# An attention pair on one Trainium2 core: half of each next unit's x loaded one step earlier, in named seats

## The chip, the cores and the metric

The kernel runs on one core of a Trainium2 chip. The metric is device time in microseconds of one execution. Each execution's profile also gives a span, from the first to the last instruction, which is a little shorter than the time.

## The reference

Two attention layers run side by side on inputs of their own, and their outputs are concatenated on the last axis. Each has x of 2048 rows by 1024 columns, a weight wqkv (1024 x 3072), 32 heads of 32 columns, and an output weight wo (1024 x 1024). Everything is float32.

- Layer B: each row attends to itself and the 255 rows before it. `softmax(q k^T / sqrt(32) + mask) v`, then `@ wo`.
- Layer A: each row attends to 8 rows: itself and the rows 2, 4, ..., 14 before it (window 8, dilation 2); then `@ wo`.

## The kernel before

**Units.** The rows are cut into 8 units of 512 rows: units 0 to 3 are layer B's, units 4 to 7 layer A's (whose rows are sorted by parity, so that the dilation becomes a plain window). In each unit the 32 heads go in 8 groups of four, s = 0 to 7. For a unit u and a group s the work is

- `qk(u, s)`: q and k of four heads, two products of 8 steps each (steps over the 1024 columns in pieces of 128),
- attention of the group: scores, row maximum, exponential, sum, values,
- `v(u, part)`: the values' product, in three parts after s = 0, 5 and 7; part 2 (16 steps) comes behind `qk(u, 7)` and is the last reader of the unit's x,
- `o(u, n)`: output projections n = 0 to 7, each contracting the outputs of all eight groups. Those of a layer B unit run in the unit behind it, two each ahead of groups 2 to 5. Those of unit 3 run in units 4 and 5, by the table `O_LATE`. The projections of layer A, and part of its values, run as a Strassen-like product of seven (`PRODUCTS`).

**Precision.** A float32 operand is split into a high part (a cast to a shorter format, lines 247 and 250) and a low part (the rest, a subtraction on VectorE, line 253). A product is three matmuls: high by high, high by low, low by high (`TERMS`). All matmuls are issued at line 295. So every tile of x or of a weight costs one cast, on ScalarE or VectorE, and subtractions on VectorE.

**The stream.** x and the weights are 512 KB items in one list, `items`, loaded in that order into three `raw` buffers (line 192, issued by POOL) and then split into `wpool` (three weight tiles) or x tiles. A raw buffer is filled again when the item three places ahead of the new one has been split. An x item makes two x tiles of 128 partitions by 2 x 512, one unit has eight. There are nine x tiles in rotation (`xpool`) and ten room tiles r0 to r9 (`slot`), which hold attention outputs by `hg % 10` (hg = 8u + s), two late x items of unit 0, and sums later on. `split_to(n)` asks for items up to n to be split. A product asks for the weight after its own at step `ASK` = 2, if that item is no x.

**The order of all instructions** is set while the program is written, by a list scheduler at the end of the function. It keeps four sequences (auxiliary rows, second scores with values, first scores, and `gemm`, the big products in the order of `plan`) and a clock model for each engine (`Clock`); it takes the next instruction group from the sequence that is ready first, and `defer` places follow-up work by modelled times. What the engines wait for on the chip is then semaphores, in the fixed order.

**x at a unit's end.** `x_items(u)` are four steps of no cost that ask for the split of the unit's four x items. They are put among the steps of other products: for unit 1 two of them in `v(0, 2)` and two in `qk(0, 7)`; for units 2 to 6 all four in part 2 of the values of the unit in front, after steps 1, 5, 9 and 13. In the list of items they stand behind the two weights of that part and the first weight of `qk(u, 0)`; the second weight of `qk(u, 0)` stands behind x.

**The start.** `FIRST` lists the pieces of the first six items (four of x, two weights); all nine loads are issued by ScalarE (lines 174 and 177). Ten matmuls on zeros (`WARM`) run before the data is there, and `FILL` puts 1, 9, 1 and 4 more behind steps 1 to 4 of the first product.

**Layer A's evacuation** (`evac_window`): q goes to SBUF at line 550, k at line 555, with 8 columns of the unit in front ahead of k: copied from `tails` by ScalarE (line 558) where there is a unit in front in the same row order, else cleared by VectorE (line 561).

## Time and profile before

| what | value |
|---|---|
| time, median of 3 runs | 1806.21 us (1802.6 to 1809.89) |
| the profiled execution: time | 1805.51 us |
| the profiled execution: span | 1803.8 us |
| TensorE matmuls busy | 1779.3 us, 14505 instructions |
| VectorE busy | 1305.3 us |
| ScalarE busy | 929.7 us |
| POOL busy | 412.1 us |
| granted TensorE clock, mean | 0.999 |
| HBM read, written | 201.33 MB, 53.48 MB |

PE is TensorE's matmul row, PEld its weight loads, DVE VectorE, ACT ScalarE, POOL GpSimd, SP the sync engine. A row of the timeline gives the start and the length in us, the engine, the line, the operation, the tile written and those read, the count, and in brackets the idle time before it and what ended it. Matmuls overlap in the pipeline, so a row of several is shorter than the sum of its instructions. A POOL row of a load is its issue, not the transfer. By the timeline unit 2 begins at about 444 us, units 3 to 7 at 700, 956, 1155, 1335 and 1518; from 1675 on only the last products run.

### The profile page before, as it was taken

What the parts mean: (1) busy time and instruction counts of PE and PEld (TensorE: products, weight loads), DVE (VectorE), ACT (ScalarE), POOL (GpSimd) and SP (SyncE); (2) the same over time, 40 slices, a digit from 0 to 9 for tenths busy, and PEclk for the clock granted to TensorE, in tenths of its full rate; (3) what the DMA queues carried; (4) which work ended last, traced back from release to release, by engine and by line L of the source; (5) the groups of instructions that cost most, each with busy time, mean ns of one, the idle gap of its engine ahead of it and who ended that gap; (6) DMA issues with size and microseconds to landing.
All of it is one profiled execution on the core that took longest, in us unless ns stands there. A gap on an engine that the chain in (4) does not pass through costs nothing.

```text
span 1803.8 us, 38475 instructions
## 1 busy us (share of the span) xinstructions
PE 1779.3 (99%) x14505; PEld 1441.8 (80%) x14505; DVE 1305.3 (72%) x2905; ACT 929.7 (52%) x2310; POOL 412.1 (23%) x951
## 2 busy tenths in 40 slices
PE   9999999999999999999999999999999999999999
PEld 7787777888777888777887778888878787887887
DVE  6777876768867769867678576665766768678866
ACT  4565566555656565656655444423443435356442
POOL 3222323222242223332223400110011101002120
PEclk9999999999999999999999999999999999999999
DMA  8354664644646556455546365675566558858984
GB/s 246 111 151 135 185 166 135 173 139 133 185 140 175 150 135 172 142 158 140 149 115 184 93 196 182 204 207 162 187 210 209 179 185 266 262 177 281 342 288 145
DMA packets 154794, 324.58 MB, mean 180 GB/s; under 512 B 18032, under 2 KB 58992, under 8 KB 154608
## 3 DMA queue, kind: packets, MB, share of 16 engines
q0 software_dynamic: 45792, 166.74, 30.5%
q1 hardware_dynamic: 97728, 134.40, 26.3%
q10 hardware_dynamic: 11088, 20.98, 3.1%
q8 instruction: 115, 1.88, 0.4%
q14 instruction: 71, 0.58, 0.1%
HBM read 201.33 MB, written 53.48 MB: 141 GB/s over the span
## 4 chain that ended last, share of the span: by engine, by line
PE 88%; DVE 4%; issue 3%; DMA 2%; ACT 2%; ACTq 0%; POOL 0%; SPq 0%; POOLq 0%; DVEq 0%
PE g L295 69%; PE s L295 13%; PE o L295 6%; DVE w L253 1%; DMA raw<-xs 1%; DMA raw<-wo 1%; DVE x L253 0%; ACT s L1351 0%; ACT w L247 0%; DMA outs<-ost 0%; ACT wide L1213 0%; DVE band L1174 0%; DMA raw<-wqk 0%; DVE band L1202 0%; DMA qst<-nat 0%
## 5 line engine op out<-in xcount | busy, mean ns | idle before, releaser
L295 PE MATMUL g<-x,w 128*128 128x512 f32 x3552 | 878.6, 393 | 6.1 <-ACT w L247 3.2
L295 PEld LDWEIGHTS g<-x,w 128*128 128x128 f32 x3552 | 654.8, 188 | 137.9 <-issue 6.3
L253 DVE TENSOR_TENSOR w<-raw,w 128x512 fp32r<-128x512 f32 x510 | 334.8, 698 | 47.9 <-ACT w L247 39.1
L1351 ACT ACTIVATE s<-s,nm 128x384 f32<-128x384 f32 (+2 forms) x512 | 274.5, 537 | 106.3 <-DVE nm L1346 100.0
L1346 DVE CUSTOM_DVE_ANT_0 s<-s,mask_d 128x384 f32<-128x384 f32 (+2 forms) x512 | 261.9, 554 | 91.6 <-PE s L295 91.3
L295 PE MATMUL g<-w,x 128*128 128x256 f32 (+1 forms) x1728 | 307.7, 327 | 1.1 <-DVE w L253 0.8
L1410 POOL TENSOR_SCALAR_AFFINE_SELECT pbuf<-pbuf 128x128 f32<-128x128 f32 (+1 forms) x603 | 220.5, 394 | 316.1 <-ACT pbuf L1431 314.2
L295 PEld LDWEIGHTS g<-w,x 128*128 128x128 f32 x1728 | 255.4, 190 | 25.7 <-issue 1.6
L295 PE MATMUL g<-r,w 128*128 128x512 f32 x960 | 239.8, 394 | 1.4 <-ACT r L1306 0.7
L1431 ACT ACTIVATE pbuf<-s 128x384 f32<-128x384 f32 (+2 forms) x480 | 203.3, 505 | 64.6 <-PE s L295 59.8
L295 PEld LDWEIGHTS g<-r,w 128*128 128x128 f32 x960 | 177.0, 188 | 37.4 <-DVE r L1310 1.6
L192 POOL DMA_DIRECT2D raw<-wqk x126 | 68.3, 542 | 406.7 <-DVE w L253 251.8
L295 PEld LDWEIGHTS s<-qst,kst 128*128 128x128 f32 x704 | 113.4, 188 | 42.3 <-ACT s L1351 16.8
L295 PE MATMUL s<-kst,qst 96*128 96x384 f32 (+2 forms) x512 | 142.9, 343 | 0.9 <-ACT s L1351 0.7
L295 PE MATMUL s<-qst,kst 128*128 128x256 f32 (+2 forms) x704 | 137.0, 302 | 4.0 <-ACT s L1351 3.2
L250 DVE CAST w<-raw 128x1024 fp32r<-128x1024 f32 x180 | 124.4, 691 | 19.7 <-PE g L295 19.6
L247 ACT CAST w<-raw 128x1024 fp32r<-128x1024 f32 (+1 forms) x76 | 78.6, 1037 | 84.1 <-PE g L295 32.9
L295 PEld LDWEIGHTS s<-kst,qst 96*128 96x128 f32 x512 | 93.5, 189 | 26.5 <-issue 4.6
L1351 ACT ACTIVATION_READ_ACCUMULATOR s<-s,nm 128x1 f32 x512 | 105.3, 206 | 0.0
L1213 ACT COPY wide<-band 32x512 f32<-32x512 f32 x128 | 79.0, 617 | 40.3 <-DVE band L1204 38.5
L295 PE MATMUL o<-pbuf,vbuf 128*32 128x384 f32 (+2 forms) x1408 | 91.6, 389 | 0.0
L591 ACT ACTIVATE nat<-g 128x512 fp32r<-128x512 f32 x64 | 38.4, 599 | 97.8 <-PE g L295 88.7
(90 smaller groups left out, 1434.0 us busy)
## 6 DMA issues: line engine op xcount, KB each, us to landing
raw<-wqk POOLq DMA_DIRECT2D x126, 512.0 KB, 4.7
raw<-wv POOLq DMA_DIRECT2D x60, 512.0 KB, 4.8
qst<-nat SPq DMA_DIRECT2D x96, 256.0 KB, 4.1
kst<-nat SPq DMA_DIRECT2D x96, 256.0 KB, 5.5
raw<-wo POOLq DMA_DIRECT2D x44, 512.0 KB, 4.7
raw<-xs POOLq DMA_DIRECT2D x28, 512.0 KB, 5.0
outs<-ost ACTq DMA_DIRECT2D x38, 256.0 KB, 2.3
kst<-halo SPq DMA_DIRECT2D x72, 128.0 KB, 4.5
```

Source lines behind the costliest of these rows:

```text
L192: (self.nc.scalar if early else self.nc.gpsimd).dma_start(raw if len(ap.shape) == 2 else raw.rearrange("p (a b) -> p a b", a=2), ap)
L247: nc.scalar.copy(t[:, 0, :], raw)
L250: nc.vector.tensor_copy(t[:, 0, :], raw)
L253: nc.vector.tensor_tensor(t[:, 1, c:c + 512], raw[:, c:c + 512], t[:, 0, c:c + 512].bitcast(F32), op=ALU.subtract)
L295: nc.tensor.matmul(out, left, right, **k)
L591: nc.scalar.activation(hl[:, 0, :], ps, AF.Copy, scale=sc)
L1213: nc.scalar.copy(diag[r:r + 32, :, :, c:c + 32], turned[r:r + 32, :, :, 1, :])
L1346: nc.vector.tensor_tensor_reduce(ps[:, :n], ps[:, :n], mask[:, cut:full], scale=-1.0, scalar=BIG, op0=ALU.add, op1=ALU.min, accum_out=nm)
L1351: nc.scalar.activation(ps[:, :n], ps[:, :n], AF.Exp, bias=nm, scale=-1.0, accum_out=sm)
L1410: nc.gpsimd.affine_select(w, w, pattern=[[0, m], [step, n]], compare_op=ALU.is_ge, fill=0.0, base=base, channel_multiplier=chan)
L1431: nc.scalar.activation(w, ps[:, :pack * n].rearrange("p (j n) -> p j n", j=pack), AF.Exp)
```

## The change

- **x earlier in layer B.** `EARLY_X` moves x items 0 and 1 of units 2 and 3, and item 0 of unit 4, ahead in the list, in front of the weights of the last value part; their splits go into `qk(u, 7)` at its steps 5 and 11 (`EARLY_AT`). The rest stays in the value part, at steps given by `LATE_AT`. As the last weight of `qk(u, 7)` now has x behind it, the first value weight is asked for by a step of its own, 13 (`ASK_V`). Unit 1's two early items stay.
- **Seats.** The x tiles of units 0 to 3 (`X_SEATS`) and the outputs of layer B (`O_SEATS`) have named tiles, out of the same nine x and ten room tiles; layer A's x goes round the nine in the order of `X_RING`. The values of the seventh group of unit 0 wait for the last qk of that unit (its output takes an x tile's seat).
- **Unit 4:** `O_LATE` puts the projections 0 to 3 of unit 3 one group later.
- **Units 5 and 6:** the second weight of `qk(u, 0)` stands between x items 1 and 2. Units 5 to 7 ask for it at step 2 of the first product of `qk(u, 0)`, when x is split.
- **The start:** loads 0 and 2 of the nine stay on ScalarE's queue (`BY_ACT`), seven go to SP; `FILL` is 1 and 5 matmuls behind steps 1 and 2.
- **Tails:** cleared once by POOL, and copied for every unit of layer A; where the next unit has none in front, VectorE clears them after use.
- One ask in front of the seven-part products comes at step 5 in place of 6.

```diff
--- before.py
+++ after.py
@@ -36,7 +36,12 @@
 XAT = 1
-FIRST_X = 2
+EARLY_X = {1: (0, 1), 2: (0, 1), 3: (0, 1), 4: (0,)}
+EARLY_AT, ASK_V = (5, 11), 13
+LATE_AT = {2: {2: 5, 3: 9}, 3: {2: 10, 3: 14}, 4: {1: 3, 2: 10, 3: 14}}
+X_SEATS = ("x0 x1 x2 x3 r0 r2 r1 r4", "x4 x5 x6 x7 x8 x0 x1 x2", "x3 r8 r9 r0 x4 x5 x6 x7", "x2 x8 r2 r3 x3 x4 x5 x6")
+O_SEATS = ("r5 r6 r3 r7 r8 r9 r0 r2", "r1 r4 r5 r6 r3 r7 r2 x8", "x0 x1 r1 r4 r5 r6 r7 r8", "r9 r0 r1 r4 r5 r6 r7 r8")
+X_RING = "x0 x1 x7 x2 x8 x3 x4 x5 x6"
 X1_AT = (2, 9)
@@ -46,7 +51,7 @@
 OUTPUT_OPS = ((3, 2, 3, ALU.add), (2, 0, 2, ALU.subtract), (0, 3, 0, ALU.subtract), (1, 1, 0, ALU.subtract))
-O_LATE = {4: {2: (0, 1), 3: (2, 3)}, 5: {2: (4, 5), 3: (6, 7)}}
+O_LATE = {4: {3: (0, 1), 4: (2, 3)}, 5: {2: (4, 5), 3: (6, 7)}}
 O_AT = {}
@@ -56,7 +61,8 @@
 FIRST = ((0, 0), (1, 0), (0, 1), (2, None), (3, 0), (1, 1), (4, None), (3, 1), (5, None))
-FILL = ((1, 1), (2, 9), (3, 1), (4, 4))
+BY_ACT = (0, 2)
+FILL = ((1, 1), (2, 5))

@@ -167,15 +173,16 @@
                 self.raw[3 + i] = raw, [None, None]
-            for i, h in FIRST:
+            for n, (i, h) in enumerate(FIRST):
                 raw, t = self.raw[i]
                 ap = self.items[i][1]
+                queue, took = (self.nc.scalar, self.ck.load) if n in BY_ACT else (self.nc.sync, self.ck.copy)
                 if h is None:
-                    self.nc.scalar.dma_start(raw.rearrange("p (a b) -> p a b", a=2), ap)
-                    t[:] = [self.ck.load("first", self.ck.now)] * 2
+                    queue.dma_start(raw.rearrange("p (a b) -> p a b", a=2), ap)
+                    t[:] = [took("first", self.ck.now)] * 2
                 else:
-                    self.nc.scalar.dma_start(raw[:, S * h:S * h + S], ap[:, h] if len(ap.shape) == 3 else ap[:, S * h:S * h + S])
-                    t[h] = self.ck.load("half", self.ck.now)
+                    queue.dma_start(raw[:, S * h:S * h + S], ap[:, h] if len(ap.shape) == 3 else ap[:, S * h:S * h + S])
+                    t[h] = took("half", self.ck.now)
             self.loaded = 6
@@ -220,7 +227,7 @@
                 for h in range(2):
-                    t = self.xpool.tile([P, 2, S], F32R, tag="x", name="x") if self.items[i][0] != "xw" else self.sums()
+                    t = self.x_tile(i, h) if self.items[i][0] != "xw" else self.sums()
                     self.ready[i].append(self.parts(t, raw[:, h * S:(h + 1) * S], t0, i < SIDE))
@@ -232,11 +239,6 @@
             self.ck.defer(end, lambda n=i + m + NRAW + 1 if i < NRAW else max(2 * NRAW + m, i + NRAW + deep + 1): self.load_to(n))
-
-    def x_tile(self, i, h):
-        if (i, h) in self.first:
-            return self.slot(self.first[i, h])
-        return self.xpool.tile([P, 2, S], F32R, tag="x", name="x")

@@ -271,7 +273,7 @@
     wpool = ctx.enter_context(tc.tile_pool(name="wpool", bufs=3))
-    xpool = ctx.enter_context(tc.tile_pool(name="xpool", bufs=NX))
+    xpool = ctx.enter_context(tc.tile_pool(name="xpool", bufs=1))
     roomp = ctx.enter_context(tc.tile_pool(name="roomp", bufs=1))
@@ -396,7 +398,7 @@
                     if i == 1 and p[1:] == (0, 2):
-                        unit_x(1, *range(FIRST_X)) if FIRST_X else None
+                        unit_x(1, *EARLY_X[1])
                 else:
@@ -404,10 +406,17 @@
                     item(p + (t,), "w", wqk[ly, 2 * p[2] + t])
+            if 0 < p[1] < DU and p[2] == NG - 1:
+                unit_x(p[1] + 1, *EARLY_X[p[1] + 1])
         else:
...
                 item(("qk", p[1], 0, 0), "w", wqk[units[p[1]][0], 0])
-                unit_x(p[1], *range(FIRST_X if p[1] == 1 else 0, 4))
+                if DU < p[1] < U - 1:
+                    unit_x(p[1], 0, 1)
+                    item(("qk", p[1], 0, 1), "w", wqk[units[p[1]][0], 1])
+                    unit_x(p[1], 2, 3)
+                else:
+                    unit_x(p[1], *[g for g in range(4) if g not in EARLY_X.get(p[1], ())])
             else:
@@ -430,8 +439,21 @@
     st.sums = sums_tile
-    st.first = {(4, 0): 6, (4, 1): 7, (5, 0): 8, (5, 1): 9}
-    st.slot = lambda i: slot(i).rearrange("p (a s) -> p a s", a=2).bitcast(F32R)
+    def place_of(name):
+        if name[0] == "x":
+            return xpool.tile([P, 2, S], F32R, tag=name, name="x")
+        return roomp.tile([P, 1024], F32, tag=name, name="r").rearrange("p (a s) -> p a s", a=2).bitcast(F32R)
+
+    ring = X_RING.split()
+    x_at = {(where["x", u, g], h): X_SEATS[u].split()[2 * g + h] for u in range(DU) for g in range(4) for h in range(2)}
+
+    def x_tile(i, h):
+        if (i, h) in x_at:
+            return place_of(x_at[i, h])
+        ring.append(ring.pop(0))
+        return place_of(ring[-1])
+
+    st.x_tile = x_tile
     last_dense = DU * NG - 1
@@ -471,6 +493,7 @@
                                 base=-8, channel_multiplier=0)
+        nc.gpsimd.memset(tails, 0.0)
         cst["keep_f"] = bands("keep_f", P, BIG, 0.0, (-1, -1, 1))
@@ -554,12 +577,10 @@
                 e = ck.use("act", 0.485, ck.now + ck.SEM)
-                if has_halo:
-                    nc.scalar.copy(qk[:, S:S + 8], tails[:, s, :])
-                    e = ck.use("act", 0.2, e)
-                else:
-                    nc.vector.memset(qk[:, S:S + 8], 0.0)
-                    ck.use("dve", 0.08, ck.now)
+                nc.scalar.copy(qk[:, S:S + 8], tails[:, s, :])
+                e = ck.use("act", 0.2, e)
+                if u + 1 < U and not units[u + 1][3]:
+                    ck.defer(e + 1.0, lambda: (nc.vector.memset(tails[:, s, :], 0.0), ck.use("dve", 0.08, ck.now)))
                 if u + 1 < U and units[u + 1][3]:
@@ -654,12 +675,16 @@
                 then = where["qk", u, s, t] + 1
+                if t == 1 and s == 0 and u:
+                    then = max(then, st.split)
                 kinds = [kind for kind, _ in st.items[then:then + 2]]
...
                     st.split_to(then + 1)
+                if k == ASK and t == 0 and u > DU and kinds[:1] == ["x"] and st.split >= where["qk", u, s, 1]:
+                    st.split_to(where["qk", u, s, 1] + 1)
                 if kinds[:1] == ["xw"] and k in (0, 2, 4, 6):
                     st.split_to(then + 1 + k // 2)
-                if kinds == ["w", "w"] and k == 6 and (then in firsts or then + 1 in firsts):
+                if kinds == ["w", "w"] and k == 5 and (then in firsts or then + 1 in firsts):
                     st.split_to(then + 2)
@@ -1301,7 +1326,7 @@
             return
-        o = slot(hg).rearrange("p (a s) -> p a s", a=2).bitcast(F32R)
+        o = place_of(O_SEATS[u].split()[s])
         ot[u, s] = o
@@ -1455,6 +1480,8 @@
             if ks[-1] == nk - 1 and hg >= NO and ((hg - NO) // NG, NG - 1) not in done["out"]:
+                return None
+            if hg == NG - 2 and (u, NG - 1) not in done["stack"]:
                 return None
@@ -1527,16 +1554,25 @@
                         new += q[2 * i:2 * i + 2] + k[2 * i:2 * i + 2]
+            if 0 < p[1] < DU and p[2] == NG - 1:
+                x1 = x_items(p[1] + 1)
+                v0 = where["v", p[1], 2, 0] + 1
+                new[ASK_V:ASK_V] = [(lambda: 0.0, lambda v0=v0: st.split_to(v0), 0.0, lambda: None)]
+                for g in reversed(EARLY_X[p[1] + 1]):
+                    new[EARLY_AT[g]:EARLY_AT[g]] = x1[g]
             if p[1:] == (0, NG - 1):
                 x1 = x1 or x_items(1)
-                for g in range(3, FIRST_X - 1, -1):
+                for g in (3, 2):
                     new[NK + 2 * g - 2:NK + 2 * g - 2] = x1[g]
...
             new = v_items(p[1], p[2])
-            if p[1:] == (0, 2) and FIRST_X:
+            if 0 < p[1] < DU and p[2] == 2:
+                for g, k in sorted(LATE_AT[p[1] + 1].items(), reverse=True):
+                    new[k:k] = x1[g]
+            elif p[1:] == (0, 2):
                 x1 = x_items(1)
-                for g in range(FIRST_X - 1, -1, -1):
+                for g in (1, 0):
                     new[X1_AT[g]:X1_AT[g]] = x1[g]
...
                 m = 2 * VPARTS[p[2]][1]

```

## Prediction

> **What bounds the kernel now.** First the page, its part 1 (busy time by engine) and part 4 (the chain of work that ended last):
>
> ```profile
> span 1803.8 us, 38475 instructions
> PE 1779.3 (99%) x14505; PEld 1441.8 (80%) x14505; DVE 1305.3 (72%) x2905; ACT 929.7 (52%) x2310; POOL 412.1 (23%) x951
> PE 88%; DVE 4%; issue 3%; DMA 2%; ACT 2%; ACTq 0%; POOL 0%; SPq 0%; POOLq 0%; DVEq 0%
> ```
>
> TensorE is the bound: it works 1779.3 of 1803.8 us and holds 88% of the chain. The program takes 1805.51 us in this execution, 1.7 us more than its span and 0.7 us under the median of the runs, 1806.21. No edit of the change removes a product of the reference, so it can win only two things: the 24.5 us in which TensorE stands still (1803.8 − 1779.3), and filler matmuls. Busy time by stretch shows where TensorE stands still; the columns are the stretch, its length, and busy us (with counts) of PE, PEld, DVE, ACT and POOL, then the granted clock, DMA share and GB/s:
>
> ```profile
> 0.00:20.00 20.00, 18.14 (x68) 14.05 (x69) 10.78 (x17) 7.42 (x12) 10.54 (x30) 1.00 0.72 248
> 20.00:1020.00 1000.00, 993.44 (x6022) 802.61 (x6024) 752.48 (x1942) 584.75 (x1687) 301.97 (x740) 1.00 0.55 151
> 1020.00:1660.00 640.00, 628.67 (x7781) 511.25 (x7774) 437.39 (x779) 281.28 (x529) 75.65 (x139) 1.00 0.65 203
> ```
>
> Layer B (20 to 1020 us) loses 6.6 us in 1000, layer A's attention (1020 to 1660) 11.3 in 640, the start 1.9, and what is left, 4.7, lies in the last products after 1660. The change touches the first three. Half a per cent, about what a measurement of this kernel can tell from no change, is 9.0 us: faster means under 1797.2, slower over 1815.2.
>
> **The start (load order, queues, fillers).** From the timeline:
>
> ```profile
> 1.53 4.63 PE L295 MATMUL s<-qst 128*128 128x512 f32 x10 [1.53 <-DVE qst L1559]
> 5.04 0.75 ACTq L174 DMA_DIRECT2D pbuf<-xs  x1
> 5.83 0.62 ACT L247 CAST w<-raw 128x512 fp32r<-128x512 f32 x1 [3.73 <-DMA raw<-wqk]
> 6.50 1.25 PE L295 MATMUL g<-x,w 128*128 128x512 f32 x3 [0.34 <-ACT w L247]
> 8.59 2.23 PE L295 MATMUL s<-qst 128*128 128x512 f32 x9
> 8.71 1.14 ACT L247 CAST x<-raw 128x512 fp32r<-128x512 f32 x2 [1.74 <-DMA raw<-xs]
> 13.90 1.29 DVE L253 TENSOR_TENSOR r<-pbuf,r 128x512 fp32r<-128x512 f32 x2
> 15.87 5.60 PE L295 MATMUL g<-r,w 128*128 128x512 f32 x24
> ```
>
> Ten warming matmuls end at 6.16. The first real one follows at 6.50, after a cast of w that ScalarE begins at 5.83, because its queue issues nine loads, the last until 5.79. With seven of them on SP, ScalarE is free by about 2 and the cast waits for the data alone, so the 0.34 us should go; no more, since the warming matmuls stay. From 6.50 to 21.47 TensorE has no idle time above 0.3 us, but 15 of its matmuls are fillers; the change leaves 6. A matmul costs 0.233 us here (5.60 / 24), nine cost 2.1 us, so at most 2.4 is won. What is late next? The third group of x: its two halves are cast from 8.71 to 9.85, the first by 9.28, while nine fillers hold TensorE until 10.82. With four fillers fewer and 0.34 won it is there at 9.5, still behind the cast; I leave 0.2 us for a wait on the second half or a subtraction. The last x halves are ready at 15.19; 12 matmuls (2.8 us) are left, which allows an end at 18.0, and by count it becomes 21.47 − 2.4 = 19.1: the loads do not bind. I take **−2.2**; bounds −2.8 (loads also earlier) and −1.0 (SP loads landing a microsecond later).
>
> ```profile
> 6.00:11.00 5.00, 4.66 (x19) 3.47 (x19) 3.13 (x5) 3.15 (x6) 3.84 (x11) 1.00 0.91 342
> ```
>
> The DMA engines are 91% busy from 6 to 11 us. The Trainium skill, "DMA: Bandwidth & Descriptors", section "Issuing engines are not separate DMA queues", says the queues share the same 16 engines, so that a second issuer saves only issue time; the busy share agrees. By it the last x lands hardly earlier and the −2.8 end is out; if a second queue brought bandwidth, −2.8 would stand. The −2.2 needs neither.
>
> **The boundaries of layer B.** The stall after unit 1, the 20 us around it and its two like (after units 2 and 3), the split of a half x tile (cast and subtraction), and VectorE ahead of the first:
>
> ```profile
> 453.13 0.82 PE L295 MATMUL s<-qst,kst 128*128 128x128 f32 x4 [0.61 <-ACT s L1351]
> 443.00:463.00 20.00, 19.08 (x127) 14.21 (x127) 18.22 (x51) 11.49 (x33) 5.48 (x10) 1.00 0.69 193
> 699.00:719.00 20.00, 19.08 (x127) 14.20 (x126) 18.39 (x51) 11.49 (x33) 5.65 (x10) 1.00 0.73 201
> 955.00:975.00 20.00, 19.39 (x128) 14.78 (x128) 18.27 (x52) 12.15 (x35) 5.33 (x10) 1.00 0.70 188
> 441.04 0.42 DVE L250 CAST x<-raw 128x512 fp32r<-128x512 f32 x1
> 441.49 0.69 DVE L253 TENSOR_TENSOR x<-raw,x 128x512 fp32r<-128x512 f32 x1
> 415.00:425.00 10.00, 10.00 (x63) 7.64 (x62) 6.56 (x17) 6.61 (x20) 0.55 (x1) 1.00 0.94 247
> 425.00:435.00 10.00, 10.00 (x67) 9.14 (x66) 9.81 (x26) 5.33 (x17) 1.82 (x3) 1.00 0.16 54
> 435.00:445.00 10.00, 10.00 (x77) 9.82 (x77) 9.79 (x21) 3.76 (x9) 5.69 (x12) 1.00 0.65 192
> ```
>
> VectorE is 98% busy from 425 to 445, because the eight x halves, 1.11 us each or 8.9 us, come together; softmax rows queue behind them, and TensorE waits for ScalarE's exponentials. It idles 0.92 + 0.92 + 0.61 = 2.4 us of the three stretches. The change takes four halves (two before unit 4) 10 to 20 us earlier, into time like 415 to 425, where VectorE is 66% busy. Named seats make this possible; each early seat (r8, r9, r0, x3; x2, x8, r2, r3; x0, x1) held an attention output whose eight projections are done by slot 5 of the unit in front, or an x tile of the unit before that. So the write need not wait. The number of loads and splits stays. VectorE is still over 90% busy in all three stretches after the x halves too, so not all goes: **−1.5** of 2.4, with +10.7 (the slower rival) and −2.4 as ends. Unit 0 loaded half of unit 1's x early already; the condition on its seventh head delays one group of value matmuls, others cover it: 0.
>
> **Projections one slot later in unit 4.**
>
> ```profile
> 1029.73 0.49 PE L295 MATMUL g<-r,w 128*128 128x512 f32 x1 [0.69 <-ACT r L1306]
> 1030.45 1.89 PE L295 MATMUL g<-r,w 128*128 128x512 f32 x7 [0.23 <-DVE r L1310]
> ```
>
> Here projection 0 of unit 3 waits 0.69 + 0.23 us for the last head's output. In the new plan 48 matmuls of unit 4's third projection pair (11 us) come first; they need x and w alone. **−0.9**; ends 0 and −0.9.
>
> **Layer A: second weight ahead of x, and asked for early.** Unit 6:
>
> ```profile
> 1326.74 0.53 POOL L192 DMA_DIRECT2D raw<-xs  x1 [3.59 <-DVE band L1174]
> 1328.87 0.53 POOL L192 DMA_DIRECT2D raw<-wqk  x1 [1.60 <-DVE x L253]
> raw<-xs POOLq DMA_DIRECT2D x28, 512.0 KB, 5.0
> 1334.61 5.63 PE L295 MATMUL g<-x,w 128*128 128x512 f32 x24
> 1341.40 1.03 ACT L247 CAST w<-raw 128x1024 fp32r<-128x1024 f32 x1
> 1342.48 3.75 PE L295 MATMUL g<-x,w 128*128 128x512 f32 x14 [2.24 <-ACT w L247]
> ```
>
> The second qk weight is fetched at 1328.87 but cast only at 1341.40: nobody asks for it until the first 24 matmuls are through, behind which ScalarE evacuates and takes exponentials. TensorE waits 2.24 us. The change puts the weight between x pairs, so it is split before 1334.6. The last x moves one load later, from the issue at 1326.74 to 1328.87, lands by the page's median of 5.0 us at 1333.9, and is needed, split, at 1334.61 + 18 × 0.233 = 1338.8: covered. **−2.2**. Units 5 and 7:
>
> ```profile
> 1148.18 0.53 POOL L192 DMA_DIRECT2D raw<-xs  x1 [0.42 <-DVE x L253]
> 1154.38 0.53 POOL L192 DMA_DIRECT2D raw<-wqk  x1 [5.67 <-DVE x L253]
> 1155.07 5.74 PE L295 MATMUL g<-x,w 128*128 128x512 f32 x24
> 1163.01 5.92 PE L295 MATMUL g<-x,w 128*128 128x512 f32 x24 [0.61 <-DVE w L250]
> 1527.23 1.05 ACT L247 CAST w<-raw 128x1024 fp32r<-128x1024 f32 x1
> 1528.33 1.92 PE L295 MATMUL g<-x,w 128*128 128x512 f32 x6 [0.58 <-ACT w L247]
> ```
>
> In unit 5 the 0.61 at 1163.01 goes the same way. But the last x, issued at 1148.18, moves to the issue at 1154.38, which waits for a split; landing at 1159.4 and split 1.1 later, 1160.5; it is needed at 1155.07 + 4.2 = 1159.3. That costs about 1.1 to 1.2 against the 0.61 won: **+0.5**, ends −0.6 and +2. Unit 7 keeps its order but asks earlier: of 0.58 I take **−0.5**.
>
> **The rest.**
>
> ```profile
> L558 ACT COPY nat<-tails 128x8 f32<-128x8 f32 x16 | 3.2, 199 | 0.2
> ```
>
> ScalarE copies tails in 16 more places, 16 × 0.2 = 3.2 us, while it is busy 281 of 640 us there; 0, or 0.2 in a few seats where a head's copy waits for it, up to +1. Half of the 16 VectorE memsets go. One memset on POOL at the start and the split at step 5 instead of 6: 0. The order of the whole stream is planned anew; no row prices that, the nearest being the stretches after units 1 and 2, whose idle time is equal to 0.01 us under equal plans, and the 11.3 us that layer A's attention loses under another. I take 0 and ±2.
>
> The sum: −2.2 − 1.5 − 0.9 − 2.2 + 0.5 − 0.5 = −6.8, so 1805.5 − 6.8 = **1798.7 us**.
>
> **The rivals.** (1) *The stalls at the boundaries stay*, since VectorE is the bound there and the early halves only move its queue; unit 5 costs its full 2. Then −2.2 − 0.9 − 2.2 + 2 − 0.5 = −3.8: 1801.7. For it speaks VectorE's 98%, against it the 66% just before. That the early x comes no earlier in fact, a seat being held, is part of this.
>
> (2) *More follows.* With units 5 to 7 relieved, their other waits (11.3 us in all there) shrink by half of what is left, about 4, and the boundaries give all 2.4: −11.7, 1793.8.
>
> (3) *Slower: the value weight becomes late.* Place: the head of the value product at each boundary, three times. Its first weight is now asked for three steps (9 matmuls, 2.1 us) ahead of use, and splitting it takes 2.0 on VectorE: the cast below and two subtractions, 1.29 at 13.90 above.
>
> ```profile
> 1162.18 0.68 DVE L250 CAST w<-raw 128x1024 fp32r<-128x1024 f32 x1
> ```
>
> Four x halves (4.4 us) now stand in VectorE's queue before it. If none of them is done by the asking, TensorE waits 4.4 − 0.1 = 4.3 twice and 2.1 at unit 4: 10.7 in place of −1.5, so −5.3 + 10.7 = +5.4, 1810.9. It decides from 1.8 us of lateness at each boundary. Against it: the first pair is put 8 steps ahead of the asking.
>
> (4) *The clock falls back at the start.* The ten warming matmuls took 4.63 us, twice 0.233 each: the array starts at half rate. If fewer fillers let it fall back, ten of the matmuls after them cost double, 2.3 us, and the start gives +0.1: 1801.0. Against it: by the steps above no wait there should be over 1 us. The Trainium skill, "TensorE: Matmul & The Clock Gate", section "What's actually happening", lets the clock drop after an idle window of about 3.4 us; the trace has no such idle piece to test it. By it this rival does not happen.
>
> (5) *No gain in all*: what TensorE wins is given back at the next wait for loads or softmax, 1805.
>
> **How the numbers follow.** Forecast 0.42, rivals (1) 0.20, (2) 0.15, (3) 0.12, (4) 0.04, (5) 0.07. The forecast's own range is 1796 to 1802 (the ±2 of the order and the terms' ends). For 8 in 10 I need (1), (4), (5), and the near half of (2): 1793.5 to 1807; left out are (3) and the rest of (2). Under 1797.2 lie (2) and a third of the forecast: 0.30. Over 1815.2 lies (3) with more mishap than its price: 0.06. Within: 0.64.
>
> **What would show it.** The start: real matmuls at 6.2, the 24 matmuls of 15.87 over by 19.5 instead of 21.47. Boundaries: x casts in the last qk pair of each unit, VectorE below 95% after, the waits for exponentials near 450, 706 and 960 gone. Unit 4: no wait for an output. Unit 6: the second weight cast before the first product ends. Unit 5: a short wait for x. I am wrong if TensorE waits at the head of a value product, if a cast waits for a seat, or if a new stall over 3 us stands anywhere.

## The result and the profile after

The changed kernel took 1813.12 us (median of 6 runs, 1810.81 to 1814.95) against 1805.42 for the kernel before (6 runs): 1.0036 times as long, 95% interval 1.0025 to 1.0047. The forecast was 1798.7, range 1793.5 to 1807. The profiled execution took 1812.9 us with a span of 1811.2; TensorE's matmuls were busy 1782.4 us and its granted clock was 0.997. It was 1803.8 us, 1779.3 us and 0.999 before.

To see where the 7.4 us of span came in, one event is followed through both traces: the row in which ScalarE takes the last k product of a unit, `qk(u, 7)`, out of PSUM. First before, then after (timeline of ScalarE, units 1 to 3):

```profile
429.90 0.60 ACT L591 ACTIVATE nat<-g 128x512 fp32r<-128x512 f32 x1 [0.17 <-PE g L295]
685.90 0.60 ACT L591 ACTIVATE nat<-g 128x512 fp32r<-128x512 f32 x1 [0.17 <-PE g L295]
941.92 0.60 ACT L591 ACTIVATE nat<-g 128x512 fp32r<-128x512 f32 x1 [0.17 <-PE g L295]
```

```profile
429.88 0.60 ACT L612 ACTIVATE nat<-g 128x512 fp32r<-128x512 f32 x1 [0.90 <-PE g L297]
691.03 0.60 ACT L612 ACTIVATE nat<-g 128x512 fp32r<-128x512 f32 x1 [0.90 <-PE g L297]
953.38 0.60 ACT L612 ACTIVATE nat<-g 128x512 fp32r<-128x512 f32 x1 [0.97 <-PE g L297]
```

At the end of unit 1 both are level (-0.02). Unit 2 loses 5.1 us and unit 3 another 6.3: +11.5. Then it falls: +9.8 at the end of unit 4, +8.9 unit 5, +5.2 unit 6, +9.8 unit 7, +7.4 at the end. So the loss lies at the first two boundaries in layer B, part of it is won back in layer A, and the start has won nothing.

Not all of the loss is TensorE standing still. Unit 2 from event to event, before and after (columns: the stretch, its length, then busy us of PE, PEld, DVE, ACT, POOL, clock, DMA share, GB/s):

```profile
429.90:685.90 256.00, 254.81 (x1578) 206.94 (x1578) 192.65 (x487) 150.99 (x431) 78.84 (x195) 1.00 0.56 155
429.88:691.03 261.15, 257.15 (x1577) 207.03 (x1576) 190.61 (x482) 150.39 (x432) 75.45 (x200) 1.00 0.55 152
```

TensorE stands still 4.0 us in place of 1.2, and is busy 2.3 us longer for the same products. That second part is scores. Four of them, for example, start at 453.33, 453.77, 454.34 and 454.90, in the end at the pace of ScalarE's exponentials (0.56 us apart there), where two at 449.99 before start 0.17 us apart; such short waits are hidden in the busy time, because the matmuls overlap. In unit 3 one window at half clock, 694.53 to 697.94, is in the loss as well, up to 1.7 us (an estimate: half of its 3.41).

**The start** after (timeline): the wait for the cast that was to go, the 24 matmuls of 15.87 before, then POOL, SP and TensorE.

```profile
6.07 1.31 PE L297 MATMUL g<-x,w 128*128 128x512 f32 x3 [0.37 <-ACT w L249]
14.16 5.60 PE L297 MATMUL g<-r,w 128*128 128x512 f32 x24
8.63 0.68 POOL L199 DMA_DIRECT2D raw<-wqk  x1 [8.12 <-DVE x L255]
10.38 0.23 POOL L478 MEMSET keep_d<- 128x128 f32 x1
21.00 1.60 POOL L199 DMA_DIRECT2D raw<-wv  x2 [0.25 <-issue]
26.49 5.80 SPq L636 DMA_DIRECT2D qst<-nat  x3
33.32 0.63 PE L297 MATMUL s<-kst,qst 96*128 96x128 f32 x4 [1.41 <-DMA kst<-nat]
```

The first matmul comes 0.43 us earlier, and the 24 matmuls 1.71. But POOL issues a load at 8.63, waiting on VectorE, ahead of its constants, which start at 10.38. The value weights go out at 21.00, SP's stores for q jam for 5.8 us at 26.49, and at 33.32 TensorE waits 1.41 us for k: the gain is gone. The cause is in the diff: the new loop `for n, (i, h) in enumerate(FIRST)` uses the name of the function's argument `n`. Behind the loop `n` is 8 and no longer 6, so two more weights are loaded at once (fix_n below tests it).

**The boundary** after unit 1 (timeline, VectorE and TensorE; the last two rows are TensorE's later waits, the second the same place after unit 2):

```profile
426.54 0.69 DVE L255 TENSOR_TENSOR r<-raw,r 128x512 fp32r<-128x512 f32 x1
429.68 0.69 DVE L252 CAST w<-raw 128x1024 fp32r<-128x1024 f32 x1
430.40 1.29 DVE L255 TENSOR_TENSOR w<-raw,w 128x512 fp32r<-128x512 f32 x2
431.09 1.57 PE L297 MATMUL s<-kst,qst 96*128 96x384 f32 x3 [1.19 <-ACT s L1376]
432.50 0.77 PE L297 MATMUL g<-w,x 128*128 128x256 f32 x5
466.47 0.22 PE L297 MATMUL s<-ident,hl 128*32 128x128 f32 x1 [1.55 <-DVE hl L1397]
692.24 1.57 PE L297 MATMUL s<-kst,qst 96*128 96x384 f32 x3 [1.19 <-ACT s L1376]
```

The early x (`r`) is split by 427.2. The value weight's cast comes at 429.68, its subtractions end at 431.7, and only at 432.50 does the first matmul of the value product start; before, the weight was split by 426.9 (rows in the first experiment). Against the event above (429.88) the cast is 0.20 us early; before it was 5.05 (424.85 and 429.90). In between the list scheduler has put scores ahead, and TensorE waits 1.19 us for an exponential of ScalarE to free a bank of PSUM that holds scores. The same wait stands at 692.24. The windows of the three old stalls, moved on by 2.4, 8 and 12 us, about the distance there, and the 10 us around the new wait (columns: us, then busy us of PE, PEld, DVE, ACT, POOL, clock, DMA share, GB/s):

```profile
445.40:465.40 20.00, 19.27 (x123) 13.63 (x121) 12.69 (x34) 10.52 (x30) 4.77 (x12) 1.00 0.55 147
707.00:727.00 20.00, 18.82 (x129) 13.82 (x129) 15.48 (x41) 10.98 (x31) 6.82 (x15) 1.00 0.72 197
967.00:987.00 20.00, 19.88 (x123) 16.17 (x122) 15.43 (x39) 11.19 (x33) 6.42 (x13) 1.00 0.74 179
425.00:435.00 10.00, 8.57 (x48) 7.05 (x47) 9.77 (x25) 3.09 (x10) 1.27 (x3) 1.00 0.47 151
```

VectorE has the room that was forecast (12.7 to 15.5 of 20 us, 18.3 before), but TensorE's idle time in the three only falls from 2.4 to 2.0 us, and the wait of 1.55 us at 466.47 stands just behind the first of them. New idle time lies at 425 to 435, where TensorE was busy all 10 us and is now 8.57.

**Layer A** after (unit 4, unit 6, a new wait in unit 6, unit 7):

```profile
1046.28 4.02 PE L297 MATMUL g<-r,w 128*128 128x512 f32 x17
1340.72 1.05 ACT L249 CAST w<-raw 128x1024 fp32r<-128x1024 f32 x1 [1.70 <-PE g L297]
1341.99 4.29 PE L297 MATMUL g<-x,w 128*128 128x512 f32 x18
1347.19 3.01 PE L297 MATMUL g<-x,w 128*128 128x512 f32 x12 [0.23 <-DVE x L255]
1369.75 0.66 PE L297 MATMUL o<-wide,vbuf 128*32 128x136 f32 x16 [1.52 <-issue]
1530.88 4.34 PE L297 MATMUL g<-x,w 128*128 128x512 f32 x11 [2.76 <-DVE x L255]
```

Unit 4's projections wait for nothing. In unit 6 the 2.24 us are gone; 0.23 for an x half is left. Unit 5, where a wait of about 1 us for x was forecast, has one of 0.34 at 1169.87. New are 1.52 at 1369.75, for which the trace names no cause, and 2.76 at 1530.88, the latter for an x split in unit 7, where 1.43 stood before.

### The profile page after: what moved, and what is told of

The parts are those of the page before. It is cut to its first block, busy times and chain, and to the rows that moved or that the text cites. A ratio compares the mean times of both kernels' runs of the same rounds, so it can differ in the third digit from the quotient of the medians.

```text
span 1811.2 us, 38396 instructions
## 1 busy us (share of the span) xinstructions
PE 1782.4 (98%) x14496; PEld 1442.0 (80%) x14496; DVE 1302.0 (72%) x2896; ACT 935.1 (52%) x2327; POOL 411.1 (23%) x952
## 4 chain that ended last, share of the span: by engine, by line
PE 87%; DVE 5%; DMA 3%; issue 2%; ACT 2%; POOL 0%; ACTq 0%; DVEq 0%; POOLq 0%
PE g L297 68%; PE s L297 12%; PE o L297 6%; DMA raw<-xs 1%; DVE w L255 1%; DMA kst<-nat 1%; ACT s L1376 1%; DVE x L255 1%; DVE qst L1411 0%; ACT w L249 0%; DMA raw<-wqk 0%; DVE w L252 0%; DVE band L1227 0%; DVE sm L1223 0%; DMA qst<-nat 0%
## 5 line engine op out<-in xcount | busy, mean ns | idle before, releaser
L297 PE MATMUL g<-x,w 128*128 128x512 f32 x3384 | 836.4, 394 | 5.0 <-DVE x L255 3.5
L297 PEld LDWEIGHTS g<-x,w 128*128 128x128 f32 x3384 | 626.3, 188 | 133.4 <-issue 6.0
L297 PE MATMUL g<-r,w 128*128 128x512 f32 x1128 | 289.6, 393 | 0.0
L297 PE MATMUL g<-w,x 128*128 128x256 f32 (+1 forms) x1548 | 275.2, 328 | 0.9 <-DVE w L255 0.6
L297 PEld LDWEIGHTS g<-w,x 128*128 128x128 f32 x1548 | 229.4, 190 | 25.4 <-DVE w L255 2.0
L297 PEld LDWEIGHTS g<-r,w 128*128 128x128 f32 x1128 | 207.2, 188 | 36.4 <-issue 0.2
L249 ACT CAST w<-raw 128x1024 fp32r<-128x1024 f32 (+1 forms) x80 | 82.8, 1038 | 72.3 <-PE g L297 30.3
L297 PE MATMUL g<-w,r 128*128 128x512 f32 (+1 forms) x516 | 105.8, 352 | 2.0 <-DVE w L255 1.0
L297 PEld LDWEIGHTS g<-w,r 128*128 128x128 f32 x516 | 84.0, 193 | 14.0 <-issue 1.9
```

The lines of the kernel that those rows point to most:

```text
L249: nc.scalar.copy(t[:, 0, :], raw)
L297: nc.tensor.matmul(out, left, right, **k)
```

## The experiments

Theory at the outset: TensorE lost its time to the value weight that is asked for at step 13. The rivals: VectorE has no room for early x; or each new order of the whole stream has its own luck. Each experiment ran beside the kernel before on one chip, four chips in all; the kernel before had medians of 1805.15 to 1807.38 us there, so kernels of different chips are compared by their ratios. The distances in the table are those of the event above from the kernel before, in profiled executions.

| kernel | median us | ratio, 95% interval | end of unit 1 | 2 | 3 | 4 | 6 | end |
|---|---|---|---|---|---|---|---|---|
| the change | 1813.12 | 1.0025 to 1.0047 | 0.0 | +5.1 | +11.5 | +9.8 | +5.2 | +7.4 |
| fix_n | 1814.21 | 1.0027 to 1.0053 | -1.6 | +5.0 | +10.3 | +8.6 | +3.9 | +4.5 |
| late_ask | 1824.55 | 1.0098 to 1.0124 | +1.7 | +6.7 | +11.6 | +19.1 | +17.1 | +18.0 |
| ask9 | 1798.19 | 0.9946 to 0.9974 | -0.9 | -1.1 | +0.1 | -1.8 | -8.9 | -7.6 |
| ask9_fix | 1796.67 | 0.9942 to 0.9966 | -1.9 | -2.2 | -0.7 | -2.7 | -9.8 | -8.9 |
| ask7_fix | 1797.57 | 0.9937 to 0.9967 | -1.8 | -2.1 | -1.1 | -3.0 | -10.1 | -9.8 |
| ask10_fix | 1805.40 | 0.9984 to 1.0002 | -1.9 | -2.2 | +0.1 | +0.3 | -2.0 | -0.1 |
| ask11 | 1805.39 | 0.9994 to 1.0011 | -0.6 | -1.0 | +1.8 | +0.8 | -2.4 | -1.2 |
| only_early | 1818.20 | 1.0048 to 1.0078 | +0.1 | +6.7 | +13.1 | +11.5 | +12.3 | +12.8 |
| early9 | 1815.86 | 1.0043 to 1.0070 | +0.9 | +0.6 | +1.7 | +8.7 | +10.0 | +10.3 |
| early9_late | 1808.18 | 1.0001 to 1.0022 | -0.5 | -0.8 | -0.1 | -1.0 | +1.5 | +2.5 |
| no_early | 1805.65 | 0.9990 to 1.0009 | +1.5 | +1.6 | +7.2 | +4.0 | +1.2 | +1.5 |
| no_early_fix | 1805.66 | 0.9988 to 1.0005 | -0.2 | -0.1 | +5.6 | +1.4 | -1.8 | -1.6 |
| no_early_913 | 1802.77 | 0.9969 to 0.9993 | -1.6 | -1.7 | -1.8 | -1.7 | -4.3 | -1.5 |
| layer_a | 1817.11 | 1.0048 to 1.0079 | +1.6 | +1.5 | +7.2 | +6.9 | +4.1 | +14.1 |
| layer_a_913 | 1814.12 | 1.0032 to 1.0059 | +1.8 | +1.8 | +3.1 | +3.0 | +0.9 | +10.1 |

The distances hold the clock too, so they are best read from one column to the next. late_ask, early9, no_early, no_early_fix and layer_a have a window at half clock near 171 us, which the first column shows (up to 1.7 us each, an estimate as above). In layer_a_913 the full clock was first granted at 10.96 us, in the other traces at 4.6 to 7.7; nine fillers took 2.71 us there and 2.23 in the kernel before, and the 1.8 us of its first column are there at 17.7 us already.

### The late ask alone, in the kernel before: late_ask

```diff
-                if k == ASK and kinds and kinds[0] not in ("x", "xw"):
+                if k == ASK and kinds and kinds[0] not in ("x", "xw") and not (0 < u < DU and s == NG - 1 and t):
...
+            if 0 < p[1] < DU and p[2] == NG - 1:
+                v0 = where["v", p[1], 2, 0] + 1
+                new[13:13] = [(lambda: 0.0, lambda v0=v0: st.split_to(v0), 0.0, lambda: None)]
```

> The kernel before with one thing of the change: the value weight that follows the last q/k product of units 1 to 3 is asked for at step 13 in place of 10, with no early x ahead of it. Theory A (what costs is a late ask behind early splits): alone it has its 2.0 us of split just covered by the three steps left, so 0 to 1 us per boundary, 1805 to 1808. Rival (the late ask alone does the harm, whatever stands ahead): 1813 or more.

1824.55 us, the slowest of all: the rival's side. Timeline of late_ask, VectorE's cast of the weight and TensorE's waits, with the same split before ahead of it:

```profile
424.85 0.68 DVE L250 CAST w<-raw 128x1024 fp32r<-128x1024 f32 x1
425.57 1.29 DVE L253 TENSOR_TENSOR w<-raw,w 128x512 fp32r<-128x512 f32 x2
```

```profile
432.14 0.69 DVE L250 CAST w<-raw 128x1024 fp32r<-128x1024 f32 x1
433.69 1.57 PE L295 MATMUL g<-w,x 128*128 128x256 f32 x11 [0.42 <-DVE w L253]
443.98 0.45 PE L295 MATMUL s<-kst,qst 96*128 96x384 f32 x1 [1.18 <-ACT s L1351]
467.79 0.22 PE L295 MATMUL s<-ident,hl 128*32 128x128 f32 x1 [1.47 <-DVE hl L1372]
```

The weight is cast 0.5 us behind the event of the table (431.64 here), where it was 5.05 ahead. TensorE waits 0.42 us for its second half, behind the product's first matmul, and later 1.18 and 1.47 for softmax, since scores were put ahead. This costs 4.9 us in unit 2 and 5.0 in unit 3: about as much as the whole change loses there (5.1 and 6.3). Unit 4 loses another 7.5, with a wait of 2.28 us that early9 shows too (below). So no early x need stand ahead of the weight; the theory's half "behind early splits" falls, its other half holds.

### Asking earlier in the changed kernel: ask9, ask11, ask9_fix, ask7_fix, ask10_fix

```diff
-EARLY_AT, ASK_V = (5, 11), 13
+EARLY_AT, ASK_V = (5, 11), 9
```

The others have 11, 7 and 10 there, and those with "fix" also the edit of fix_n below. Since items are split in order, an ask ahead of step 11 pulls the second early x with it.

> The changed kernel, asking for the first value weight at step 9 of the last qk pair instead of 13. Theory A (TensorE has no product to work on at 430 and 691 us since the value weight is late): the waits of 1.2 us at both places vanish, the clock does not drop at 694, 1806 to 1809. Theory B (VectorE has no room in any order, the x splits stand ahead of the row maxima): the waits stay or move to the row maxima, 1812 to 1814.

> The changed kernel with the value weight asked for at step 11 in place of 13: two steps, about 1.4 us of TensorE, earlier. Theory A (lateness of the weight is what costs): the price falls with the lateness. At step 13 TensorE was 1.2 us short of a product at 431, so two steps earlier it is just covered: the waits at 431 and 692 go and the time is near that of step 9, 1798 to 1802. Theory B (step 9 merely drew a better order of the whole stream, and each plan has its own luck): no order between 9, 11 and 13; a time above 1806 or waits at 431 and 692 that stay.

> The changed kernel with the value weight asked for at step 9 and the loop variable at the start renamed, so that the two early weight loads go back behind the constants. Theory (the start's loss to the jammed queues adds to the late weight): the 1.5 us that the rename kept through unit 1 are kept to the end as well: 1796.5 to 1797.5. Rival (what is won at the start is only moved to the next wait, as with the rename alone): as with step 9 alone, 1798.2 within 1 us, with other waits behind 33 us.

> The changed kernel with the renamed loop variable and the value weight asked for at step 7 in place of 9 (1796.67). Theory A (only lateness costs): at step 9 nothing waits for that weight any more, so nothing more is won: 1795.5 to 1798. Theory B (each plan has its own luck in units 2 to 4, the ask merely draws another): anything from 1794 to 1806, with waits in places that neither step 9 nor 13 had.

> The changed kernel with the renamed loop variable and the value weight asked for at step 10, the step it has in the kernel before. Theory A (lateness is what costs): at step 9 nothing waited, at 11 it cost some 8 us; at step 10 the split still ends before the last product ends, so 1796 to 1799. Theory B (each plan has its own luck): above 1800.

Timeline of the weight's split and the head of the value product, ask9_fix and then ask11:

```profile
424.63 0.69 DVE L252 CAST w<-raw 128x1024 fp32r<-128x1024 f32 x1
427.85 2.31 PE L297 MATMUL g<-w,x 128*128 128x256 f32 x18
```

```profile
426.59 0.69 DVE L252 CAST w<-raw 128x1024 fp32r<-128x1024 f32 x1
429.09 2.31 PE L297 MATMUL g<-w,x 128*128 128x256 f32 x18
```

With every ask from 7 to 11 the weight is split when the product starts, and the waits at 431 and 692 are gone. Unit 2 costs -0.2 to -0.4 us against before in all five, in place of +5.1, and unit 3 +1.0 to +2.7 in place of +6.3. That far the theory is shown; ask9 gained more than it had said. The totals, though, stand on two levels: 1797 to 1798 for 7 and 9, 1805 for 10 and 11, which both missed what was expected. ask9, ask9_fix and ask7_fix have TensorE's instructions in one and the same order to the end. ask10_fix is equal to ask9_fix within 0.04 us until 685 us and has another order from about 704 us on. ask10_fix at the third boundary:

```profile
968.77 2.53 PE L297 MATMUL g<-x,w 128*128 128x512 f32 x9 [0.82 <-DVE w L252]
973.41 0.94 PE L297 MATMUL s<-kst,qst 96*128 96x384 f32 x4 [2.12 <-DMA kst<-nat]
```

Here TensorE waits 0.82 us for another weight's cast and 2.12 us for the transfer of k into `kst`. At the end of unit 4 it is 2.9 us behind ask9_fix, at the end of unit 6 7.8. That is another order of the whole stream, drawn by one step: the rival holds for units 3 to 7.

### The renamed variable: fix_n

```diff
-            for n, (i, h) in enumerate(FIRST):
+            for at, (i, h) in enumerate(FIRST):
...
-                queue, took = (self.nc.scalar, self.ck.load) if n in BY_ACT else (self.nc.sync, self.ck.copy)
+                queue, took = (self.nc.scalar, self.ck.load) if at in BY_ACT else (self.nc.sync, self.ck.copy)
```

> The changed kernel, with one name mended: the loop over the nine first loads counts in n, which is also the limit up to which loads are asked for; n is 8 after the loop, so that two more loads are issued on POOL before the constants are built. Theory (the two loads hold POOL's constants and the value weights behind them, and the 1.7 us won by 20 us are given back at 33 us for that): the first value weight is issued near 10 instead of 21, no wait for kst at 33, 1.5 to 2 us under the changed kernel, near 1811.4. Rival (the loads themselves are the limit at 30 us, in whatever order): the wait at 33 stays and the time is the changed kernel's, 1813.

```profile
31.32 0.56 PE L297 MATMUL s<-kst,qst 96*128 96x128 f32 x4
31.46 1.85 SPq L636 DMA_DIRECT2D kst<-nat  x3
```

The row of 33.32 has become one of 31.32 with no wait, and the lead of 1.6 us stays to the end of unit 1. So the two loads were the cause. The median did not follow (1814.21, 1811.4 expected); the profiled execution, the fastest of its five (1810.07), is ahead of the change's to the end (+4.5, +7.4), and the others ran at clocks of 0.995 to 0.997. With step 9 the profiled executions are 1.3 us apart at the end (-8.9, -7.6); the medians, 1796.67 and 1798.19, are of two chips, and their intervals overlap.

### Early x without the rest: only_early, early9, early9_late

only_early is the kernel before with early x and the seats; early9 asks at step 9; early9_late has the shift of the projections too:

```diff
-O_LATE = {4: {2: (0, 1), 3: (2, 3)}, 5: {2: (4, 5), 3: (6, 7)}}
+O_LATE = {4: {3: (0, 1), 4: (2, 3)}, 5: {2: (4, 5), 3: (6, 7)}}
```

> The kernel before with early x for units 2 to 4 and the named seats alone; start, projections of unit 3, tails and layer A's order as before. Theory (early x costs 11.4 us): 1815 to 1818. Rival (early x is harmless, the loss lies in the start and layer A): 1804 to 1806.

> The kernel before with the early x and the shared seats alone (start, unit 4's projections and layer A as before), and the value weight asked for at step 9. It was 1818.2 with step 13. Theory A: the 13 us above the kernel before are all the late weight, so they go: 1803 to 1806, and early x itself is worth 0 to -2. Theory B (the early splits themselves fill VectorE): it stays above 1810.

> The kernel before with the early x, the shared seats, the value weight at step 9 and, added to the run before this one, the change's one-slot shift of unit 3's projections in unit 4. That run lost 8 us against the kernel before between the end of unit 3 and the third q/k product of unit 4, with a wait of 2.28 and one of 0.68 us and two windows of half clock. Theory (the projections stood too close behind the last head, and early x alone pushes that head back): those 8 us go, 1806 to 1809. Rival (the seats or the early x of unit 4 cost them, whatever the projections do): 1813 or more.

only_early came out 0.2 us above what the theory said. The earlier ask takes away what is lost in units 2 and 3 (+13.1 becomes +1.7), but early9 missed its 1803 to 1806: it loses 7 us in unit 4. There its timeline has

```profile
1034.20 1.85 PE L297 MATMUL o<-pbuf,vbuf 128*32 128x256 f32 x16 [2.27 <-POOL pbuf L1434]
1036.74 1.52 PE L297 MATMUL g<-r,w 128*128 128x512 f32 x2 [0.68 <-ACT r L1330]
```

a wait for the last head's attention on POOL and one for its output, and from 1034.32 two windows at half clock (up to 3.4 us of the 7). It isn't early x by itself that pushes that head back: late_ask, without early x, has the same waits (2.28 and 0.69), and only_early, with it, wins 1.6 us in unit 4. In early9_late the projections wait for nothing, and the 7 us are gone, as expected:

```profile
1033.94 4.24 PE L297 MATMUL g<-r,w 128*128 128x512 f32 x18
```

### The rest without early x: no_early, no_early_fix, no_early_913, layer_a, layer_a_913

```diff
-EARLY_X = {1: (0, 1), 2: (0, 1), 3: (0, 1), 4: (0,)}
+EARLY_X = {1: (0, 1), 2: (), 3: (), 4: ()}
...
-LATE_AT = {2: {2: 5, 3: 9}, 3: {2: 10, 3: 14}, 4: {1: 3, 2: 10, 3: 14}}
+LATE_AT = {2: {0: 1, 1: 5, 2: 9, 3: 13}, 3: {0: 1, 1: 5, 2: 10, 3: 14}, 4: {0: 1, 1: 5, 2: 10, 3: 14}}
...
```

The names with "913" have the steps 1, 5, 9, 13 in all three units, as the kernel before. layer_a keeps the old start, projections and tails; what is left is the layer A part and the seats.

> The changed kernel with x of units 2, 3 and 4 split in the value part again, behind the two value weights, as before the change; the named seats and everything else stay. Theory (early x is what costs: 11.4 us from 430 to 953 us of the trace): 1801 to 1803, faster than before by 3. Rival (the seats, or the new orders elsewhere, cost): 1810 or more.

> The changed kernel with the renamed loop variable and without early x for units 2 to 4 (so their value weight is asked for at step 10, as before): start, shifted projections, layer A and seats remain. Theory (early x has a worth of its own, once the weight is not late): 1801 to 1804.5, some 5 us above the same kernel with early x and step 9 (1796.67). Rival (early x is worth nothing, and the rest of the change makes the whole gain): 1796 to 1798.

> As the run of the changed kernel without early x and with the renamed variable (1805.66), but with the third and fourth x of units 3 and 4 split at steps 9 and 13 as in the kernel before, not 10 and 14. Theory (those two places lost the 5.3 us at the head of unit 3, by order alone): 1799.5 to 1802, so that early x itself is worth some 3 to 5 us beside 1796.67. Rival (the loss comes from the missing early x or from the start): it stays at 1804 or more.

> The kernel before with the layer A part of the change alone: the second weight ahead of the second half of x in units 5 and 6, asked for early in units 5 to 7, and the weights' split at step 5. The shared seats are in, but no x is early. The forecast's own terms for it were -2.2 + 0.5 - 0.5 = -2.2: 1803.4 if they hold. From the trace of the changed kernel, whose distance from the kernel before fell from 9.8 at the end of unit 4 to 7.4 at the end: 1803. Rival (unit 5's late x eats it): 1805 or more.

> As the layer A run (1817.11), with the third and fourth x of units 3 and 4 at steps 9 and 13 as in the kernel before; what is left is the layer A part and the shared seats. Theory: the 4.8 us at unit 3 go; units 5 and 6 win some 4 us as there; the 8 us lost in the last 100 us of that run came from the order of that plan, and may stay: 1800 to 1803 without them, 1808 to 1812 with them. Rival (the layer A part loses by itself): above 1812.

All but no_early_913, which came within 1 us, took longer than the theories said. no_early, no_early_fix and layer_a lose 5.6 us in unit 3, which the steps 9 and 13 in place of 10 and 14 take away (1.4 of it stays in layer_a_913): two x splits one step later were the reason, by the order and by the clock (no_early_fix has new waits of 0.88 and 0.87 us and then half clock from 719.62 to 726.45, up to 3.4 us). no_early_913 gives the cleanest reading: -1.6 at the end of unit 1, and -1.6 to -1.8 through layer B. So the start is worth 1.6 us and keeps them. layer_a_913 gains 2.1 us in units 5 and 6 (+3.0 to +0.9), as the terms said, and then loses 9 from the end of unit 6 on, so that its time is on the rival's side (above 1812); its largest new wait there is this one, for which the trace names no cause:

```profile
1662.71 7.55 PE L297 MATMUL g<-x,w 128*128 128x512 f32 x25 [4.12 <-issue]
```

With start, tails and shifted projections in, no_early_913 loses 2.8 there, the change 2.2. Why is open.

## Why the prediction was wrong, step by step

**The boundaries of layer B (-1.5) is the step that failed**, in two ways. First, the -1.5 put the late ask of the value weight at nothing; it stood only in rival (3), with 0.12 and a price of 4.3 us at two boundaries, 10.7 in all. It came: 11.5 us at two boundaries. The seats were right ("So the write need not wait"): the early halves after unit 1 were split from 422.18 to 427.2, where the first x half was cast at 437.76 before, and no cast waited for a seat there. The argument against rival (3), that early x stands 8 steps ahead of the asking, was about the wrong thing, since late_ask pays as much with no early x. The kernel before asks at step 2 of the second product, which is step 10 of the pair; the change moves that to 13, and I priced 2.1 us of margin against 2.0 of split, without VectorE's other work and without what the scheduler does with a product that is not ready. The third boundary, priced at 2.1 us in rival (3), won 1.6, so it is in part luck that rival (3)'s 1810.9 comes near the measured time.

Second, early x itself was worth nothing in layer B. With the ask in time ask9_fix stands at -2.7 at the end of unit 4, no_early_913 at -1.7, and at the end of unit 3 it is the other way round (-0.7, -1.8). The three stalls of 0.61 us that were to go are replaced by waits of 0.60 to 1.25. That is what rival (1) said would come, but not its reason: VectorE was busy 14.5 to 16.7 of 20 us in ask9_fix's stretches, so it was no longer the bound. In whole time ask9_fix does beat no_early_913 (0.9954 and 0.9981 of the kernel before, intervals apart). That comes behind unit 4, where no x is early (units 5 and 6: -7.1 and -2.6); whether the early x or the order drawn with it makes it was not separated.

**The start (-2.2):** 1.6 us once the variable is renamed, kept to the end of unit 4 in no_early_913; none as it stands. Its steps held (0.43 for the first matmul, nine fillers less), and I took a loop variable for what it looked like. The last x was cast at 11.58 instead of 13.24 and bound nothing, as said. The DMA engines moved 397 GB/s from 6 to 11 us in place of 342:

```profile
6.00:11.00 5.00, 4.59 (x17) 3.04 (x18) 4.19 (x8) 4.04 (x9) 1.76 (x4) 1.00 1.07 397
```

Two loads of these are the misplaced ones; the six traces of kernels with the renamed variable and the new start had 370 to 382 GB/s and the last x at 11.31 to 11.50, the seven with all nine loads on ScalarE's queue 341 to 367 and 12.31 to 13.42. I had cited the Trainium skill, "DMA: Bandwidth & Descriptors", section "Issuing engines are not separate DMA queues", for loads that land hardly earlier; here the last x was cast 1.7 us earlier, though its load was issued only 0.2 us earlier (4.87 and 5.04).

**Projections in unit 4 (-0.9):** the wait is gone. Without early x the shift moves nothing measurable (no_early_913: -1.8 to -1.7). Its worth is another one: under an order that brings the last head late, as early9's, it spares 7 us, which I had not seen.

**Layer A (-2.2, +0.5, -0.5):** units 5 and 6 give -4.7 in the changed kernel (+9.8 to +5.2) against -1.7 forecast, -2.1 in layer_a_913. Unit 7 and the end give +2.2 in place of -0.5; the wait for the x split at 1530.88 (2.76, 1.43 before) and the half clock behind it are part of that. About 1.4 us of both figures is work that changed sides: six matmuls that stood ahead of unit 6's event stand behind it.

**The rest (0 ± 2):** the redrawn order is the term with the wrong size. Steps that cost nothing by themselves moved 7 us (projections), 5.6 us (two x splits by one step) and 7 to 9 us (the ask from 9 to 10, by the ratios and by the traces), half clock included. The parts do not add: by their medians early x with the late ask costs 13 us, layer A alone 7 to 11, and all of it with the ask at 9 wins 7, and 9 with the variable renamed.

**The clock** was in no term. Over the runs, span times one minus the granted clock is 6.3 us in the mean for the change and 3.5 for the kernel before (76 runs beside the experiments). So about 3 of the 7.7 us are half clock behind the new waits (last section), an estimate, since the clock is on record to 0.001, which is 1.8 us. Rival (4), a drop at the start, did not happen.

The sum for the profiled execution: 0.0 (start) + 11.5 (two boundaries) - 1.6 (third, unit 4) - 4.7 (units 5, 6) + 2.2 (unit 7 and end) = 7.4. With the ask at 9 and the variable renamed the same change gives 1796.67 us, 0.9954 times the kernel before (0.9942 to 0.9966), 2 us below the forecast; no version here is faster (ask7_fix, 0.9952, is not told apart from it). That it lies near the forecast is luck, since the terms are others: -1.9 at the start, -0.8 in the rest of layer B and unit 4, -7.1 in units 5 and 6, +0.9 from there on.

## What to carry to other kernels

When an item is put ahead of another in a stream that is prepared in order, look first at who asked for the one behind it, and when: three steps of lateness cost 5 us per boundary here, because a scheduler that fixes the order beforehand fills the hole with work that stalls later. Where such a scheduler redraws everything, local terms add up only as far as the order stays the same; follow one event per stage through both traces, and give the redrawing a range of several us. And read a diff for reused names as well as for its intent.

## What the runs showed of the hardware

The granted clock drops to half in windows of 3.41 us on a fixed grid, as a rule after a window in which TensorE was idle for about half, and at times for a third. The same wait of 2.24 us for a weight in unit 6 shows it, in the kernel before and in early9 (windows of the grid, then the wait in early9):

```profile
1338.18:1341.59 3.41, 2.06 (x10) 1.36 (x8) 2.89 (x4) 1.31 (x3) 0.00 (x0) 1.00 0.53 184
1341.59:1345.01 3.42, 2.53 (x10) 1.79 (x11) 2.48 (x5) 3.30 (x7) 0.70 (x1) 1.00 0.31 101
```

```profile
1348.35:1351.76 3.41, 1.23 (x4) 0.75 (x5) 2.12 (x4) 3.36 (x6) 0.00 (x0) 1.00 0.18 67
1351.76:1355.17 3.41, 3.41 (x9) 2.65 (x9) 3.10 (x5) 3.26 (x7) 0.72 (x1) 0.50 0.70 181
```

```profile
1350.53 1.98 PE L297 MATMUL g<-x,w 128*128 128x512 f32 x5 [2.24 <-ACT w L249]
```

Before, the wait is cut by the grid (1.35 us and 0.89 idle) and the clock (third column from the right) stays 1.00. In early9 it falls into one window, 2.18 idle, and the next runs at 0.50, which costs up to 1.7 us more (an estimate, half of 3.41). In the 17 traces, the last window of each left out, 22 of 25 windows with over 1.71 us idle were followed by one at half clock, 10 of 78 with 1.0 to 1.71, and none of some 8800 with less. The Trainium skill, "TensorE: Matmul & The Clock Gate", section "What's actually happening", has the free-running window of 3413 ns, and the traces agree; it lets the clock drop after an idle window, and here half of one was enough. So a wait of one to three us costs more in one run than in the next, and runs of one kernel differ along with it: early9's took from 1808.4 us of span at a clock of 0.999 to 1818.0 at 0.993. Why 10 windows with less idle time dropped as well is open: one wait of 0.97 and one of 0.12 us near 169, alike in most traces, fell into one window in late_ask and in ask9_fix (1.10 us idle in both), and only late_ask's next window ran at half clock.
